# r of eight tiles read in 1536-byte runs and turned by 64x64 products, rstd on ScalarE, a new order

## The chip, the core and the metric

The kernel runs on one core of one Trainium2 chip, in one launch. The metric is the device time of one execution in microseconds, lower is better. The core's engines work side by side, each through its own list of instructions in order: TensorE (PE, with its weight loads PEld), VectorE (DVE), ScalarE (ACT), GpSimd (POOL), and SyncE (SP), whose list here is only the issuing of transfers. ACT also issues a few transfers. All transfers run on the same 16 DMA engines.

## The reference

The first half is a linear attention with a decaying state over 768 time steps, for 4 batches, 8 heads and head size 48. The second half is a normalised two-layer network with a residual.

```python
for t in range(S):
    kt, vt, rt = k[:, :, t], v[:, :, t], r[:, :, t]
    cur = einsum('bhd,bhe->bhde', u[None] * kt, vt)
    y[:, :, t] = einsum('bhd,bhde->bhe', rt, state + cur)
    state = w[None, :, :, None] * state + einsum('bhd,bhe->bhde', kt, vt)
x = y.transpose(0, 2, 1, 3).reshape(B, S, 384)
xn = (x - mean(x)) / sqrt(var(x) + 1e-06) * g_ln
out = x + maximum(xn @ w_ch1, 0) @ w_ch2      # 384 -> 1536 -> 384
```

The inputs r, k, v lie in memory as (batch, head, time, 48), in float32.

## The kernel before

**Tiles.** The 768 steps of each batch are cut into 6 chunks of 128 steps. Tile i is chunk i // 4 of batch i % 4, so there are 24 tiles, and tile i needs the state that tile i - 4 left. Inside a tile the recurrence is written as products over 128 steps, with the powers of w drawn into r and k ahead of them (factor tables Fr and Fk, made once at the start from ln w and exp).

**One tile's way.** The steps are small functions, and each names its tile:

- LR, LK, LV load r, k and v of the tile as (128 tokens, 8 heads, 48), which makes 1024 runs of 192 bytes per load. SR and SK multiply by Fr and Fk into sc in bfloat16 (heads padded to 64). CV copies v to bfloat16.
- TR turns r and k on PE by products with the identity (heads in pairs, 128x128 each, four for r and four for k), and TC, TCr, TCk copy the results from PSUM into trs. For tiles 12 to 23 TKR does both by a DMA transpose instead.
- AT makes the 128x128 scores of each head (16 products of two tiles are one ATP). AM, or its halves AMa and AMb, multiplies them by the causal mask into A on DVE.
- Q multiplies the turned r by the turned k. S makes the bonus (a product with uwI) and the state's gain k^T v, and for tiles 4 to 7 adds the old state by a product with the identity. CC copies the bonus to cc, VB makes Vb = v * cc. ZU and ZD form the new state Z.
- Y makes the output from A and v, and from the turned r and the old Z. X adds Vb into x (fp32) on DVE, with the row sum. SQ squares on ACT, XN makes the centred bfloat16 xn. LT turns xn on PE and XT copies it to xT (LT2 and LTD do it by a DMA transpose). RS makes rstd.
- UP is one piece of the first layer (12 or 6 products into one PSUM bank), RL the relu into hT, DN a third of the second layer (4 products), OT the output with rstd and the residual, STO the store. DA, DB, OA, OB, SA and SB are the halves for the last tile.

Tiles 0 to 5 and 20 to 23 go through the network alone, tiles 6 to 19 in pairs (GROUPS). UP's number is 16 * group + piece.

**Weights.** LW1 loads a third of w_ch1 (768 KB, 2048-byte runs), SW scales a quarter of the columns' rows by the norm's gain and rounds it (three SW per third). LW2 and CW do the same for w_ch2 in the same buffers. LC and WF load w, u and g for the tables; WB, LN, FK, FR, CT, CP, WL build the tables. DU issues PE products on a tile of zeros.

**Order.** The scheduler is off. PLAN is one long list of steps (name, number, engine letter), and walking it fixes each engine's order: `v` is DVE, `s` ACT, `g` POOL, and h, p, o, a choose a PSUM bank. An engine that reaches an instruction whose input isn't there waits, and all that stands behind it on that engine waits too. [...]

```python
for step in PLAN.split():
    name, i, e = step.split(",")
    steps[name](int(i), e)
```

Of the kernel before, what the change touches and what calls it, by code (L numbers as in the profile page):

```python
# [19 lines left out]
DU,7,h SR,0,v TR,0,h TCk,0,s SR,1,v TR,1,h TCk,1,v TCr,0,s Q,0,v AT,0,- CP,0,s WL,0,s LR,2,- SR,2,g TCr,1,v LK,2,- SK,2,g TR,2,h AMb,0,v AMa,0,v  # L20
AT,1,- LV,1,- LK,3,- AMb,1,v AMa,1,v UW,0,g TCk,2,s TCr,2,s AT,2,- AMb,2,v UGC,0,s LV,0,- CV,0,s S,0,h CC,0,v VB,0,v ZU,0,v Y,0,h X,0,v XN,0,v LR,3,-
CV,1,s Q,1,g SK,3,g SR,3,g TR,3,- Q,2,g S,1,o CC,1,v VB,1,g ZU,1,v AMa,2,v Y,1,- X,1,v LK,5,- LR,4,- SR,4,g TCr,3,s TCk,3,s AT,3,- Q,3,v AM,3,v LV,2,-
CV,2,s S,2,h CC,2,s ZU,2,v LT,0,o XN,1,s XT,0,s LK,4,- LR,5,- SR,5,v VB,2,v SK,4,g DU,3,p TR,4,- TC,4,v Q,4,v LV,3,- CV,3,s S,3,o CC,3,s SQ,1,s ZU,3,v
LV,4,- SK,5,g TR,5,- TC,5,s VB,3,g Y,2,- X,2,v LT,1,- XT,1,s XN,2,s CV,4,g S,4,h ZU,4,v CC,4,s LV,5,- CV,5,g ATP,4,- AM,4,v LW1,0,- SW,1,s Y,3,h
SQ,0,s X,3,v XN,3,s SQ,2,s LT,2,h XT,2,v Q,5,g S,5,- AM,5,v ZU,5,v Y,4,o SW,2,g SW,0,g UP,16,- RL,16,s LW1,2,- SW,6,s CC,5,s LT,3,- XT,3,s UP,32,-
RL,32,s UP,0,- RL,0,s LW1,1,- SW,5,s VB,4,g X,4,v XN,4,v SW,7,g SW,8,g UP,2,o RL,2,v VB,5,g UP,48,p RL,48,v Y,5,h SW,3,g LK,6,- SK,6,v X,5,v UP,18,-
RL,18,s XN,5,s SW,4,g UP,49,p RL,49,s UP,33,o LR,7,- SR,7,v UP,34,- RL,34,s LK,7,- SK,7,g RS,2,g RL,33,v UP,17,- RL,17,s TR,7,p TC,7,s RS,0,g LT,5,h
XT,5,v LT,4,- UP,1,o LR,6,- Q,7,v LW2,2,- UP,82,- SR,6,g TR,6,- UP,81,- XT,4,s RL,1,v LV,7,- CV,7,v CW,5,v S,7,- CC,7,v ZU,7,v CW,4,g DN,6,- RL,82,v
# [36 lines left out]
def kernel(  # L65
# [142 lines left out]
    def LC(i, e):  # L208
        if i == 2:
            issuer(e).dma_start(out=rows[2 * HP : NR, :], in_=moe_g_ln.rearrange("(kc p) -> kc p", p=P))  # L210
# [129 lines left out]
    def CV(i, e):  # L340
        copy(e, vv(i)[:], vf(i)[:])
# [321 lines left out]
```

## Time and profile before

| what | value |
|---|---|
| times of three runs | 148.16, 148.97, 151.61 us (median 148.97) |
| profiled execution | 148.24 us, of which the profile's span is 146.5 us |
| PE busy | 135.8 us, 93% of the span |
| DVE busy | 110.5 us, 75% |
| ACT busy | 80.1 us, 55% |
| POOL busy | 94.0 us, 64% |
| DMA | 99267 packets, 94508 of them under 512 bytes; SP's queue 86.3% of 16 engines' span |
| instructions | 4250 |

An engine's busy time is the time in which at least one of its instructions was running. Matmuls overlap, so a mean duration (219 ns for a product with 128 columns) is longer than the distance from one to the next. The span starts with the first recorded instruction and ends with the last store.

### The profile page before, as it was taken

To read this page: it belongs to the slowest core of one execution; us is meant where nothing else is said; L and a number is where in the kernel's file an instruction comes from. 1 tells how busy PE (TensorE), PEld (TensorE's weight loads), DVE (VectorE), ACT (ScalarE), POOL (GpSimd) and SP (SyncE) were. 2 spreads that over 40 slices of the span, in tenths; PEclk is the share of its full clock that TensorE was granted. 3 is DMA by queue.
4 is the path that set the end of the run, shared out by engine and by line. 5 is a ranking of instruction groups with operands and counts; after the bars stand their busy time and mean duration, and the time that the engine had idled before them with its cause. 6 is when DMAs were issued, how large, how long until landed. Compare 5 with 4: busy or idle time off the path is not lost.

```text
span 146.5 us, 4250 instructions
## 1 busy us (share of the span) xinstructions
PE 135.8 (93%) x1693; PEld 108.2 (74%) x1693; DVE 110.5 (75%) x220; ACT 80.1 (55%) x175; POOL 94.0 (64%) x132
## 2 busy tenths in 40 slices
PE   3966699999999999999999999999999999999991
PEld 1455477998687897787688887966877777888871
DVE  4569999767969899985959948897946796875232
ACT  2575577977676467466386560663654752244600
POOL 4089878967888999989957493428553076644030
PEclk9999556999999999999999999999999999999999
DMA  5999899999889999899999999988999997830114
GB/s 97 209 211 221 175 277 401 194 258 380 231 170 188 206 197 232 156 215 242 96 229 206 260 233 186 217 166 185 245 157 199 229 184 156 206 123 0 54 37 182
DMA packets 99267, 28.59 MB, mean 195 GB/s; under 512 B 94508, under 2 KB 97712, under 8 KB 99248
## 3 DMA queue, kind: packets, MB, share of 16 engines
q1 hardware_dynamic: 98352, 27.24, 86.3%
q10 hardware_dynamic: 896, 1.09, 2.0%
q8 instruction: 13, 0.21, 0.6%
q14 instruction: 6, 0.05, 0.1%
HBM read 18.88 MB, written 4.72 MB: 161 GB/s over the span
## 4 chain that ended last, share of the span: by engine, by line
PE 60%; SPq 11%; DMA 11%; DVE 7%; POOL 6%; issue 4%; DVEq 0%; POOLq 0%
PE hp L527 17%; PE o L557 16%; PE s L557 7%; PE s L527 5%; SPq L332 4%; DMA w_f<-in_moe_w_ch_dram 4%; SPq L329 4%; SPq L326 3%; DMA trs<-sc 3%; DMA rf<-in_r_dram 3%; PE o L527 3%; PE at L371 2%; PE hp L452 2%; POOL sc L194 2%; PE at L348 2%
## 5 line engine op out<-in xcount | busy, mean ns | idle before, releaser
L527 PEld LDWEIGHTS <-w_sb 128*128 128x128 bf16 x612 | 47.9, 114 | 2.4 <-POOL w_sb L312 0.4
L527 PE MATMUL hp<-xT,w_sb 128*128 128x128 bf16 (+1 forms) x408 | 39.9, 244 | 0.3 <-POOL w_sb L312 0.3
L557 PEld LDWEIGHTS <-hT 128*128 128x128 bf16 x276 | 25.2, 97 | 13.7 <-issue 0.4
L557 PE MATMUL o<-w_sb,hT 128*128 128x384 bf16 x180 | 34.5, 326 | 0.0
L543 ACT ACTIVATE hT<-hp 128x512 bf16<-128x512 f32 x41 | 24.3, 597 | 18.2 <-PE hp L527 17.7
L381 DVE TENSOR_TENSOR A<-at,mask 128x1024 bf16<-128x1024 f32 (+1 forms) x27 | 28.9, 1096 | 1.2 <-PE at L371 1.2
L194 POOL TENSOR_TENSOR sc<-kf,Fk 128x384 bf16<-128x384 f32 x14 | 14.5, 1044 | 10.5 <-DMA kf<-in_k_dram 10.4
L434 POOL TENSOR_TENSOR Vb<-vf,cc 128x384 f32<-128x384 f32 x17 | 14.7, 868 | 8.7 <-ACT cc L189 3.6
L557 PE MATMUL s<-w_sb,hT 128*128 128x384 bf16 x96 | 18.9, 326 | 0.2 <-DVE x L459 0.2
L194 POOL TENSOR_TENSOR q<-trs 128x512 bf16<-128x512 bf16 x11 | 13.4, 1220 | 5.5 <-PE hp L527 2.6
L194 POOL TENSOR_TENSOR sc<-rf,Fr 128x384 bf16<-128x384 f32 x12 | 13.0, 1082 | 5.3 <-DMA rf<-in_r_dram 5.3
L466 ACT ACTIVATE sqj<-x,sm 128x384 bf16<-128x384 f32 x24 | 14.7, 611 | 1.4 <-DVE x L459 1.3
L615 DVE SCALAR_TENSOR_TENSOR ot<-o,rs,x 128x384 f32<-128x384 f32 x15 | 9.2, 613 | 4.5 <-POOL rs L483 2.8
L459 DVE SCALAR_TENSOR_TENSOR x<-hp,Vb 128x384 f32<-128x384 f32 x19 | 10.5, 554 | 2.3 <-PE hp L452 1.6
L483 POOL TENSOR_TENSOR rs<-rs,expo 128x1 f32<-128x1 f32 (+1 forms) x17 | 10.6, 625 | 1.4
L472 ACT ACTIVATE xn<-x,sm 128x384 bf16<-128x384 f32 x13 | 8.0, 613 | 5.7 <-DVE x L459 5.6
L371 PE MATMUL at<-trs 48*128 48x128 bf16 x192 | 8.6, 229 | 2.4 <-ACT trs L189 1.2
L527 PE MATMUL s<-xT,w_sb 128*128 128x128 bf16 (+1 forms) x120 | 10.8, 235 | 0.0
L194 POOL TENSOR_TENSOR Z<-ZS,WLZ 128x384 bf16<-128x384 f32 x10 | 10.3, 1030 | 0.6 <-DVE ZS L428 0.6
L545 DVE TENSOR_SCALAR hT<-hp 128x512 bf16<-128x512 f32 x9 | 6.2, 689 | 4.6 <-PE hp L527 4.6
L371 PEld LDWEIGHTS <-trs 48*128 48x128 bf16 x192 | 6.0, 99 | 4.9 <-ACT trs L189 2.1
L194 DVE TENSOR_TENSOR sc<-rf,Fr 128x384 bf16<-128x384 f32 x12 | 7.5, 633 | 2.3 <-DMA rf<-in_r_dram 2.2
(116 smaller groups left out, 214.3 us busy)
## 6 DMA issues: line engine op xcount, KB each, us to landing
rf<-in_r_dram SPq DMA_DIRECT2D x24, 192.0 KB, 3.8
kf<-in_k_dram SPq DMA_DIRECT2D x24, 192.0 KB, 3.9
vf<-in_v_dram SPq DMA_DIRECT2D x24, 192.0 KB, 3.9
w_f<-in_moe_w_ch_dram SPq DMA_DIRECT2D x6, 768.0 KB, 7.2
out_dram<-ot SPq DMA_DIRECT2D x18, 192.0 KB, 3.4
out_dram<-ot ACTq DMA_DIRECT2D x5, 192.0 KB, 2.0
trs<-sc SPq DMA_TRANSPOSE x12, 3.9
xT<-xn SPq DMA_TRANSPOSE x9, 2.8
```

The lines of the kernel that those rows point to most:

```text
L194: engines[e].tensor_tensor(out=out, in0=in0, in1=in1, op=ALU.mult)
L371: nc.tensor.matmul(out=t[:, par, q, :], lhsT=trs(i)[p0 : p0 + D, 1, q, :], rhs=trs(i)[p0 : p0 + D, 0, q, :], start=True, stop=True,)
L381: nc.vector.tensor_tensor(out=AA(i)[:, a:b].rearrange("p e q t -> p (e q) t"), in0=psum["at", i][:, a:b].rearrange("p e q t -> p (e q) t") ...
L434: engines[e].tensor_tensor(out=Vb(i)[:].rearrange("p (h d) -> p h d", h=H), in0=vf(i)[:], in1=cc(i)[:].unsqueeze(2).to_broadcast([P, H, D] ...
L459: nc.vector.scalar_tensor_tensor(out=xx(i)[:], in0=psum["y", i][:, :C], scalar=1.0, in1=Vb(i)[:], op0=ALU.mult, op1=ALU.add, accum_out=sm[ ...
L466: nc.scalar.activation(out=sqj[:], in_=xx(i)[:], func=ACT.Square, bias=sm[i][:], scale=-float(C), accum_out=sq[g][:, j : j + 1])
L472: nc.scalar.activation(out=xn(i), in_=xx(i)[:], func=ACT.Identity, bias=sm[i][:], scale=-float(C))
L483: nc.gpsimd.tensor_tensor(out=rs[g][:], in0=rs[g][:], in1=expo[:, :n], op=ALU.pow)
L527: nc.tensor.matmul(out=t[:, a * gw : (a + 1) * gw].rearrange("p (j t) -> p j t", j=size), lhsT=w1_sb[n][kc][:, fb::FB], rhs=xT(g)[:, :size ...
L543: nc.scalar.activation(out=o, in_=s, func=ACT.Relu)
L557: nc.tensor.matmul(out=psum["o", i][:, :C], lhsT=hT(g)[:, fk, j * P : (j + 1) * P], rhs=w2_sb[d][:, a, :], start=(seen == 0 and a == 0), s ...
L615: nc.vector.scalar_tensor_tensor(out=ot(i), in0=psum["o", i][:, :C], scalar=rs[g][:, j : j + 1], in1=xx(i)[:], op0=ALU.mult, op1=ALU.add,)
```

## The change

**Loads of r for tiles 0 to 7.** LR of these tiles reads 1536-byte runs: one run is eight consecutive tokens of one head. The partition is then (group of eight tokens, head), and the free dimension is (token in the group, 48). A load has 128 runs instead of 1024. The tiles 8 to 23, and all of k and v, are loaded as before.

**Turning them.** Because a partition now holds a head, r's factor table has another layout, Fq, made once by the new steps MR, MU, MS, WS, LNQ, FA and FQ (small integer tables, a product with a selection matrix for ln w per partition, Ln, a DVE product, Exp). TR of these tiles is 32 products of 64 rows, 64 weights and 32 columns, instead of r's four 128x128 ones, into a two-bank float32 tile; TCr copies it with a permuted access pattern. k of these tiles is turned by TK (four 128x128 products) and copied by KC. The heads are paired as (q, q + 4) instead of (2q, 2q + 1) throughout, which changes access patterns in SK, SR, CV, CC and Y.

**rstd.** RS moves from POOL (a scale, then a power) to ACT (Ln with scale and bias, then Exp).

**Vb.** VB may run on ACT, as eight products of one head each; five tiles use it.

**Order.** PLAN is a new list. The products on zeros at the start (DU,21, DU,7 and DU,3) are gone, one DU,6 stands ahead of the first UP, and the first table loads come in another order.

```diff
+PACK = 8
+R_PACKED = 8
 PLAN = """
-LR,1,- LK,0,- MI,0,g MW,0,v WF,0,s WB,0,- LC,0,s LC,1,s MM,0,g MP,0,v TL,0,s LC,2,s DU,21,h LN,0,s FK,0,s FR,0,s SK,0,v LK,1,- LR,0,- SK,1,v CT,0,o
+LR,1,- MI,0,g MW,0,v LC,0,s MS,0,v WS,0,- WF,0,s WB,0,h LC,1,s LC,2,s CT,0,o MM,0,g MR,0,g MU,0,v TL,0,s LNQ,0,s FA,0,v LR,0,- MP,0,v FQ,0,s SR,1,v
...
+    def WS(i, e):
+        t = psum["wq"] = bank(e, "p", [P, 512], FP32)
+        for a in range(2):
+            nc.tensor.matmul(
+                out=t[:, :D], lhsT=sel[:, a].rearrange("k p h -> k (p h)"),
+                rhs=rows[:HP, a * DP : a * DP + D], start=(a == 0), stop=(a == 1),
+            )
+    def LNQ(i, e):
+        nc.scalar.activation(out=lnq[:], in_=psum["wq"][:, :D], func=ACT.Ln)
+    def FA(i, e):
+        times(
+            e, Fq[:], lnq[:].unsqueeze(1).to_broadcast([P, PACK, D]),
+            pow_r[:].unsqueeze(2).to_broadcast([P, PACK, D]),
+        )
+    def FQ(i, e):
+        nc.scalar.activation(out=Fq[:], in_=Fq[:], func=ACT.Exp)
...
     def LR(i, e):
+        if i >= R_PACKED:
+            issuer(e).dma_start(out=rf(i)[:], in_=chunk_src(r, i))
+            return
+        c, b = divmod(i, B)
+        issuer(e).dma_start(
+            out=rf(i)[:].rearrange("p j d -> p (j d)"),
+            in_=r[b, :, c * L : (c + 1) * L, :].rearrange("h (p j) d -> p h (j d)", j=PACK),
+        )
     def SR(i, e):
-        times(e, scr(i)[:, :, :D], rf(i)[:], Fr[:])
+        if i < R_PACKED:
+            times(e, scr(i)[:, :, :D], rf(i)[:], Fq[:])
+        else:
+            times(e, paired(scr(i))[:, :, :, :D], plain(rf(i)[:]), plain(Fr[:]))
     def TR(i, e):
...
+        t = psum["tr", i] = ps_a.tile([P, 2, 512], FP32, name="at")
+        n = PACK * HP * LP // 2
+        to = t[:, :, :n].rearrange("p g (j q t) -> p g j q t", j=PACK, q=HP)
+        for j in range(PACK):
+            for a in range(2):
+                for g in range(2):
+                    par = (g + a) % 2
+                    half = slice(g * DP, (g + 1) * DP)
+                    nc.tensor.matmul(
+                        out=to[par * DP : (par + 1) * DP, g, j],
+                        lhsT=scr(i)[half, j, :], rhs=pick[half, par],
+                        start=True, stop=True,
+                    )
+    def TK(i, e):
+        t = psum["tk", i] = bank(e, "a", [P, 2 * HP, P], BF16)
+        flat = sck(i).rearrange("p (q e) d -> p q (e d)", e=2)
+        for q in range(HP):
+            nc.tensor.transpose(out=t[:, q, :], in_=flat[:, q, :], identity=ident[:])
+    def KC(i, e):
+        copy(e, trs(i)[:, 1], psum["tk", i][:, :HP])
     def TCr(i, e):
+        if i < R_PACKED:
+            n = PACK * HP * LP // 2
+            copy(
+                e, trs(i)[:, 0].rearrange("p q (g t j) -> p g q t j", g=2, j=PACK),
+                psum["tr", i][:, :, :n].rearrange("p g (j q t) -> p g q t j", j=PACK, q=HP),
+            )
     def VB(i, e):
+        if e == "s":
+            for h in range(H):
+                nc.scalar.activation(out=o[:, h], in_=vf(i)[:, h], func=ACT.Copy, scale=cc(i)[:, h : h + 1])
     def RS(g, e):
-        nc.gpsimd.tensor_scalar(
-            out=rs[g][:], in0=sq[g][:], scalar1=1.0 / C, scalar2=1e-6 * C * C, op0=ALU.mult, op1=ALU.add
-        )
-        nc.gpsimd.tensor_tensor(out=rs[g][:], in0=rs[g][:], in1=expo[:, :n], op=ALU.pow)
+        nc.scalar.activation(out=rs[g][:], in_=sq[g][:], func=ACT.Ln, bias=eps[:], scale=1.0 / C)
+        nc.scalar.activation(out=rs[g][:], in_=rs[g][:], func=ACT.Exp, scale=-0.5)
```

Three places show how the lists move. The first is SP's list from its tenth load to the third part of w_ch1 (rf, kf, vf are the tiles of r, k, v, the number behind them is the tile; w1_f is a third of w_ch1). Before:

```order
L329 DMA rf3_83<-in_r_dram 128x8x48
L326 DMA kf5_74<-in_k_dram 128x8x48
L329 DMA rf4_84<-in_r_dram 128x8x48
L332 DMA vf2_93<-in_v_dram 128x8x48
L326 DMA kf4_73<-in_k_dram 128x8x48
L329 DMA rf5_85<-in_r_dram 128x8x48
L332 DMA vf3_94<-in_v_dram 128x8x48
L332 DMA vf4_95<-in_v_dram 128x8x48
L332 DMA vf5_96<-in_v_dram 128x8x48
L301 DMA w1_f0_243<-in_moe_w_ch1_dram 128x3x512
L301 DMA w1_f2_245<-in_moe_w_ch1_dram 128x3x512
L301 DMA w1_f1_244<-in_moe_w_ch1_dram 128x3x512
```

And of the change:

```order
L385 DMA rf3_83<-in_r_dram 128x1x384
L378 DMA kf4_73<-in_k_dram 128x8x48
L391 DMA vf1_92<-in_v_dram 128x8x48
L391 DMA vf2_93<-in_v_dram 128x8x48
L391 DMA vf3_94<-in_v_dram 128x8x48
L378 DMA kf5_74<-in_k_dram 128x8x48
L385 DMA rf5_85<-in_r_dram 128x1x384
L391 DMA vf5_96<-in_v_dram 128x8x48
L353 DMA w1_f2_251<-in_moe_w_ch1_dram 128x3x512
L353 DMA w1_f1_250<-in_moe_w_ch1_dram 128x3x512
L385 DMA rf6_86<-in_r_dram 128x1x384
L353 DMA w1_f0_249<-in_moe_w_ch1_dram 128x3x512
```

Ahead of the first third of w_ch1 stand 18 loads of 1024 runs before, and 11 of them with 6 of 128 runs in the change; v of tile 4 moved behind the weights.

The second place is DVE's first work behind the memsets, up to the first masked scores (A0 is the masked score tile of tile 0; trs0 is r and k of tile 0 turned). Before:

```order
L194 TENSOR_TENSOR sc0_102<-kf0_69,Fk_232 128x8x48
L194 TENSOR_TENSOR sc1_103<-kf1_70,Fk_232 128x8x48
L194 TENSOR_TENSOR sc0_102<-rf0_80,Fr_231 128x8x48
L194 TENSOR_TENSOR sc1_103<-rf1_81,Fr_231 128x8x48
L191 COPY trs1_113<-hp_325 128x512
L194 TENSOR_TENSOR q0_117<-trs0_112 128x512
L191 COPY trs1_113<-hp_325 128x512
L381 TENSOR_TENSOR A0_120<-at_337,mask_228 128x512 x2
```

And of the change:

```order
L206 TENSOR_TENSOR sc1_103<-rf1_81,Fq_235 128x8x48
L206 TENSOR_TENSOR sc0_102<-kf0_69,Fk_239 128x2x4x48
L203 CAST trs0_112<-at_322 128x2x4x64
L206 TENSOR_TENSOR sc2_104<-rf2_82,Fq_235 128x8x48
L203 COPY trs0_112<-s_391 128x512
L206 TENSOR_TENSOR q0_117<-trs0_112 128x512
L203 COPY trs1_113<-hp_470 128x512
L480 TENSOR_TENSOR A0_120<-at_476,mask_228 128x512 x2
```

The copies of the two turned halves of tile 0 and of k of tile 1 (L203) now stand between the products, and the first masked scores stand behind k of tile 1. On PE the turns of tiles 0, 1, 4 and 2 and k of tiles 0 and 1 stand ahead of tile 0's scores.

The third place is DVE just ahead of the first relu of the network (hT is the relu's output, x the attention's output). Before:

```order
L459 SCALAR_TENSOR_TENSOR x3_143,sm3_170<-hp_591,Vb3_139 128x384
L191 COPY xT2_159<-hp_604 128x384
L381 TENSOR_TENSOR A2_122<-at_579,mask_228 128x1024
L194 TENSOR_TENSOR Z5_133<-s_610,WLZ_241 128x384
L459 SCALAR_TENSOR_TENSOR x4_144,sm4_171<-o_622,Vb0_136 128x384
L474 TENSOR_SCALAR xn2_156<-x4_144,sm4_171 128x384
L545 TENSOR_SCALAR hT0_161<-o_694 128x4x128
```

And of the change:

```order
L480 TENSOR_TENSOR A0_120<-at_667,mask_228 128x1024
L203 CAST trs0_112<-at_679 128x2x4x64
L564 SCALAR_TENSOR_TENSOR x2_142,sm2_169<-s_716,Vb2_138 128x384
L564 SCALAR_TENSOR_TENSOR x3_143,sm3_170<-o_730,Vb3_139 128x384
L480 TENSOR_TENSOR A1_121<-at_741,mask_228 128x1024
L206 TENSOR_TENSOR Z3_131<-hp_657,WLZ_247 128x384
L480 TENSOR_TENSOR A2_122<-at_750,mask_228 128x1024
L647 TENSOR_SCALAR hT0_161<-hp_811 128x4x128
```

Before, PE's first UP (UP,16, bank hp) stands behind Y of tiles 0 to 4 and S of tiles 0 to 5. In the change the first UP (UP,2) stands behind Y of tiles 0 to 3 and S of tiles 0 to 3, and it writes bank o, which X of tile 3 (x3 above) reads.

More of the change, by code (lines that the diff above doesn't have):

```diff
@@ L21 @@
[L21 to L28, printed above, removed]
@@ L93 @@
     FB = FW // P
+    LP = L // PACK
+    assert H == PACK and H * LP == P
     assert D <= DP and H % 2 == 0 and S % L == 0 and C % P == 0 and F % (P * NW) == 0
@@ L161 @@
     one = const.tile([1, P], FP32, name="one")
-    ln_all = const.tile([P, H, D], FP32, name="ln_all")
+    ln_all = Fr
     NR = 2 * HP + CK
@@ L254, in MP @@
         nc.vector.memset(uwI[:], 0.0)
-        nc.vector.memset(expo[:], -0.5)
+        nc.vector.memset(eps[:], 1e-6 * C * C)
     def DU(i, e):
```

155 lines of the change are left out of this document (98 added, 57 removed).

## The prediction

> **What bounds the kernel now.** I read the slices of the span first, then the busy time in windows, then the chain that ended last.
>
> ```profile
> span 146.5 us, 4250 instructions
> PE   3966699999999999999999999999999999999991
> PEclk9999556999999999999999999999999999999999
> ```
>
> From the seventh slice on (22 us) PE is busy almost without a break up to the last slice. Before that it is half idle, and in slices 5 and 6 it runs at half clock. So the time is made of the moment at which the dense stretch begins, PE's own work behind it, the gaps in it, and a tail. The windows have, behind the stretch and its length, the busy time of PE, PEld, DVE, ACT and POOL (with instructions), the granted clock, the DMA share and GB/s:
>
> ```profile
> 10.00:15.00 5.00, 2.75 (x57) 2.28 (x56) 4.93 (x12) 3.22 (x9) 4.58 (x5) 0.90 1.07 210
> 15.00:20.00 5.00, 3.96 (x42) 2.97 (x43) 5.00 (x12) 2.47 (x8) 3.97 (x5) 0.50 0.89 179
> 20.00:25.00 5.00, 4.83 (x75) 3.92 (x72) 4.88 (x12) 3.94 (x10) 4.34 (x6) 0.58 1.02 381
> 25.00:30.00 5.00, 4.90 (x93) 4.91 (x94) 4.18 (x9) 4.34 (x11) 4.36 (x7) 1.00 0.96 220
> 70.00:80.00 10.00, 9.46 (x125) 7.83 (x124) 7.99 (x14) 5.72 (x16) 7.92 (x11) 1.00 1.21 177
> ```
>
> Two resources are full from 10 to 25 us: DVE (4.93, 5.00 and 4.88 of 5) and the DMA engines (1.07, 0.89 and 1.02). The window from 70 us has PE's longest idle time in the dense stretch, 0.54 us.
>
> ```profile
> 16.70 0.98 SPq L332
> 17.72 5.84 DMA w_f<-in_moe_w_ch_dram
> 25.10 0.86 PE hp L527 x12
> 142.48 1.00 PE o L574 x12
> ```
>
> The first UP (L527) starts at 25.10 us. By the chain it was released by w_ch1, whose load SP issued at 17.72 behind 18 loads. PE ends at 143.48, and the last 3.0 us of the span are one DVE product and the last store. Nothing in the change shortens that tail, since OA,23 and SA,23 still end the lists.
>
> DVE would have allowed UP only a little earlier, though. Its rows in the stretch:
>
> ```profile
> 9.64 0.41 DVE L191 COPY trs<-hp 128x512 bf16<-128x512 bf16 x1
> 9.98 3.07 DVE L381 TENSOR_TENSOR A<-at,mask 128x512 bf16<-128x512 f32 x5
> 12.97 0.15 DVE L191 COPY cc<-hp 128x8 f32<-128x8 f32 x1
> 13.15 0.56 DVE L434 TENSOR_TENSOR Vb<-vf,cc 128x384 f32<-128x384 f32 x1
> 13.63 0.55 DVE L194 TENSOR_TENSOR Z<-hp,WLZ 128x384 bf16<-128x384 f32 x1
> 14.10 0.55 DVE L459 SCALAR_TENSOR_TENSOR x<-hp,Vb 128x384 f32<-128x384 f32 x1
> 14.69 0.42 DVE L474 TENSOR_SCALAR xn<-x,sm 128x384 bf16<-128x384 f32 x1
> 16.63 0.70 DVE L194 TENSOR_TENSOR q<-trs 128x512 bf16<-128x512 bf16 x1
> 17.25 1.21 DVE L381 TENSOR_TENSOR A<-at,mask 128x1024 bf16<-128x1024 f32 x1
> 18.39 0.54 DVE L194 TENSOR_TENSOR Z<-hp,WLZ 128x384 bf16<-128x384 f32 x1
> L545 DVE TENSOR_SCALAR hT<-hp 128x512 bf16<-128x512 f32 x9 | 6.2, 689 | 4.6 <-PE hp L527 4.6
> ```
>
> From one start to the next I take the real price of a DVE step in this stretch: a half mask (12.97 - 9.98) / 5 = 0.60, Vb 0.48, Z 0.47, X 0.59, Q 0.62, a whole mask 1.14, a copy of turned k 0.41, cc 0.15.
>
> **The change part by part.**
>
> *Loads.* A load of 192 KB at the 210 GB/s of the window from 10 us takes 0.94 us. The w_ch1 loads, with 2048-byte runs, move at 381 GB/s, which would make 0.52 us for the same 192 KB; for 1536-byte runs there is no row, and the ends are 0.52 and 0.94. I take the lower, as its runs are the nearer in size. Ahead of w_ch1 six loads of r save 6 x 0.42 = 2.5 us, and v of tile 4 moves behind it (0.94), so w_ch1 is issued and lands some 3.4 us earlier. That is hidden: what is late next is DVE, worked out here.
>
> *The start of the attention.* Fq has a longer chain than Fk had:
>
> ```profile
> 0.71 0.55 ACTq L204 DMA_DIRECT2D w_row<-in_w_dram  x1
> 0.80 0.17 DVE L225 MEMSET rows<- 11x128 f32 x1 [0.80 <-PEq L647]
> 1.16 0.73 DVE L252 MEMSET sc<- 128x128 uint32 x5
> 1.91 0.38 DVE L253 MEMSET WLZ<- 128x384 f32 x1
> 2.78 1.28 ACT L230 ACT_TABLE_LOAD   x1 [2.78 <-DVE expo L255]
> 2.82 0.42 ACTq L210 DMA_DIRECT2D rows<-in_moe_g_ln_dram  x1
> 4.67 0.61 ACT L277 ACTIVATE Fk<-ln_all,pow_i 128x384 f32<-128x384 f32 x1
> 7.32 1.06 PE L348 MATMUL hp<-ident,sc 128*128 128x128 bf16 x16
> L194 POOL TENSOR_TENSOR sc<-rf,Fr 128x384 bf16<-128x384 f32 x12 | 13.0, 1082 | 5.3 <-DMA rf<-in_r_dram 5.3
> ```
>
> ACT's first issue now waits for the memset of rows (ends at 0.97 instead of a start at 0.71, +0.3), and the fourth issue (0.42) comes ahead of the table load, which therefore ends at 2.78 + 1.28 + 0.7 = 4.8. Then come Ln of 48 columns (below the 0.61 of Fk; say 0.3), FA on DVE (0.56, as Vb), FQ (0.61) and SR,0 on POOL (1.08): the first turn can start at about 7.4. The first transposes of before started at 7.32. So this part costs nothing, but the masked scores and all that follows wait for more PE work than before.
>
> *The turns.* No row shows a 64x64 product with 32 columns. The nearest:
>
> ```profile
> 22.97 0.50 PE L452 MATMUL hp<-vv,A 128*128 128x48 bf16 x8
> 32.54 0.45 PE s L348 x8
> 37.08 0.55 PE at L371 x16
> 37.63 0.76 PE s L557 x4
> 39.06 0.65 PE o L557 x4
> 40.36 0.17 PE hp L444 x4
> 40.53 0.20 PE hp L452 x8
> 42.18 0.08 PE hp L402 x4
> ```
>
> Products with 48 columns take 0.20 / 8 = 25 ns each at full clock. At half clock eight of them lasted 0.50 us, of which about 0.19 is the run-out of the last, so (0.50 - 0.19) / 7 = 44 ns. Transposes take 0.45 / 8 = 56 ns, and 16 at the start 1.06 / 16 = 66 ns. The 48-row score products (34 ns each) also show that a change of the array's shape costs something: four DN behind them took 0.76 instead of 0.65 us, 0.11 more. I take 27 ns at full clock and 44 at half, with 0.11 per turn: these turns are nearest to the 48-column products. A turn is then 32 x 0.027 + 0.11 = 0.97 us, or 32 x 0.044 + 0.11 = 1.52 us at half clock. The bounds are 25 ns below and 56 (66 at half clock) above.
>
> Ahead of the first masked score PE must do the turns of tiles 0, 1, 4 and 2 and k of tiles 0 and 1. The products on zeros that warmed the clock are gone (they ran from 3.84 us, and by 7.32 the transposes were at full rate), so I put the first two turns and the first k at half clock: 2 x 1.52 + 0.62 + 2 x 0.97 + 0.45 = 6.05. With 0.25 for the last result and 0.41 for KC,1 the first mask starts at 7.4 + 6.05 + 0.25 + 0.41 = **14.1 us, against 9.98 before**. DVE stands idle for part of that.
>
> *DVE from there to the first UP.* UP,2 writes the bank that X,3 reads, and stands on PE behind Y,3. DVE's list up to X,3: six half masks 3.60, two Vb 0.96, four X 2.36, three Z 1.41, two Q 1.24, two KC 0.82, one cc 0.15, one whole mask 1.14, one TCr from float32 PSUM (as a relu, 0.69): 12.4 us. So X,3 ends at 26.5 and UP,2 starts at about **26.7, 1.6 us later than 25.10**. ACT and POOL were less full in this stretch (2.47 and 3.97 of 5 us from 15 us), and the weights are there.
>
> *PE work behind the first UP.* Less of the attention is done by then. Added are S of tiles 4 and 5 with the old state (16 small products 4 x 0.08 / 2 = 0.16, k^T v 2 x 0.17 as the 96-column products of L444, two products of 384 columns 2 x 0.16), Y of one more tile (0.17 + 0.20), one LT (3 x 0.056 = 0.17), less 8 transposes (0.45): +0.9. The turns of tiles 6 and 7 come on top: 2 x 0.97 = 1.9. Sum **+2.8 us**, all on the engine that sets the end.
>
> *The rest.* RS on ACT, Vb on ACT and the other engine letters move work between engines that have room in the dense stretch (in the window from 70 us DVE 80%, ACT 57%, POOL 79%). I price them at nothing. Where an Ln and Exp, or eight small products, delay a relu that PE waits for, it costs up to a microsecond; where POOL's relief feeds PE sooner, up to 0.5 is won. The earlier loads end 8 x 0.42 = 3.4 us of transfer time; PE's gaps of that kind are 0.54 us at most in that window, and I leave them in.
>
> Sum, against the profiled execution's 148.24 us: 148.24 + 1.6 + 2.8 = **152.6 us**. That run lies 0.7 us below the median of the three runs shown (148.97).
>
> A rule of the Trainium skill speaks against the change. Its page "TensorEngine Tiling" (Restrictions, Key Properties) says that column tiling switches off the fast weight load and that changing the tiling mode drains the engine; "TensorE: Matmul & The Clock Gate" (LDWEIGHTS) gives columns / 1.2 ns for a plain load, by which I estimate 64 / 1.2 = 53 ns per product and 1.7 us per turn. By that the sum would be close to the first rival's. The drain agrees with the trace (0.76 against 0.65 us). The load no row here shows; the first page also says that separate tiles load and multiply in parallel, which would leave my sum as it is.
>
> **Rivals.**
>
> *Each product pays for its own load.* At the transposes' 66 and 56 ns a turn is 2.22 or 1.90 us. The first mask starts at 14.1 + 2 x 0.70 + 2 x 0.93 = 17.4, and the two later turns cost 1.9 more: 152.6 + 3.3 + 1.9 = 157.8 us. For it speaks that every product loads new weights, against it that neighbours here use different quarters of the array, as the score products use different halves (34 ns).
>
> *DVE is never starved, and the kernel isn't slower.* If the turns overlap well enough, DVE runs its list without a break from the end of its memsets (about 6.9 us: FA ends at 5.7, then the memsets of sc and WLZ, 0.73 + 0.38). Ahead of the first mask it has three products, a TCr, two KC and a Q, 3 x 0.5 + 0.69 + 0.82 + 0.62 = 3.6. So the first mask is at 10.5, UP,2 at 23.1, 2.0 earlier; with 2.7 more work for PE and the 0.5 us of waiting for transfers won the time is 148.24 - 2.0 + 2.7 - 0.5 = 148.4. For it: DVE did run unbroken from 9 to 25 us before. The point from which it decides is a first mask at 13.4 us: later than that the time is over 2% above the median. I have 14.1, so it is close.
>
> *The weights were the bound.* If UP followed w_ch1, it would start 3.4 us earlier: 148.24 - 3.4 + 2.8 = 147.6. Against it stands DVE's list, which ends no sooner than 23.1. This would be the change doing what its loads suggest.
>
> **How the numbers follow.** My forecast has 0.50, from 150.5 to 155 us with 152.6 the likeliest; the full load price 0.17, the unstarved DVE 0.25, the weights 0.03. To be faster by over 2%, which is about what a measurement of this kernel can tell from no change, UP would have to start before 20 us, below DVE's unbroken list: 0.05. A fourth of the forecast's chance (0.12) lies under 151.95, so within 2% is 0.25 + 0.03 + 0.12 = 0.40 and slower 0.55. The range goes from 148.0 to 157.6; outside it lie the weights, the faster case and the upper part of the load case, together under 0.2.
>
> **What would show it.** Right: the first mask row on DVE at about 14 us, DVE full from there to 26, the first UP at 26 to 27 and w_ch1 waiting unused from about 20; eight groups of 32 products of about 1 us. Wrong: UP before 24 us or starting just behind w_ch1's scaling, turns of 2 us and more, or a dense stretch of PE with new gaps, where relus or outputs wait for ACT.

## The result, and the profile after

| | median | lowest to highest | runs |
|---|---|---|---|
| before | 148.82 us | 148.16 to 151.61 | 4 |
| with the change | 152.27 us | 151.81 to 152.73 | 4 |

The ratio is 1.027, with a 95% interval from 1.022 to 1.032: slower. The profiled execution took 152.19 us. Ratios here and below are against the kernel before on the same chip and leave out slow executions (over 1.5% above the fastest of their kernel); the profiles of two experiments (turns issued twice, products on zeros) are of slow executions, so only rows of single groups are used from them.

The slices of the span, as for before:

```profile
span 150.4 us, 4736 instructions
PE   2777799998979999999999998999999998999992
PEclk9999999999999999999999999999999999999999
```

PE is busy from the sixth slice on, as before (whose sixth slice has a 9, too), but there are more slices below 9 behind it. Next the start, on PE (start, duration, line, shapes, count, and the idle time ahead with what ended it) and on DVE:

```profile
6.46 1.04 PE L427 MATMUL at<-pick,sc 64*64 64x32 bf16 x64 [0.82 <-POOL sc L206]
7.44 0.61 PE L437 MATMUL s<-ident,sc 128*128 128x128 bf16 x4
11.05 2.48 DVE L480 TENSOR_TENSOR A<-at,mask 128x512 bf16<-128x512 f32 x4
23.55 0.56 DVE L564 SCALAR_TENSOR_TENSOR x<-o,Vb 128x384 f32<-128x384 f32 x1
24.23 1.11 PE L629 MATMUL o<-xT,w_sb 128*128 128x128 bf16 x12
28.23 0.43 PE L427 MATMUL at<-pick,sc 64*64 64x32 bf16 x32
28.59 0.86 PE L629 MATMUL hp<-xT,w_sb 128*128 128x128 bf16 x12
```

The first two turns begin at 6.46, the first mask at 11.05, and the first UP (L629) at 24.23, behind X of tile 3 (23.55). So the dense stretch begins 0.87 us **earlier** than before (25.10). It ends at 147.45. The same stretch of before and of after, with the busy time of PE, PEld, DVE, ACT and POOL:

```profile
25.10:143.48 118.38, 117.31 (x1477) 95.34 (x1477) 90.25 (x170) 65.52 (x143) 77.11 (x102) 1.00 0.89 191
```

```profile
24.23:147.45 123.22, 119.65 (x1568) 97.12 (x1566) 97.86 (x183) 72.64 (x202) 68.90 (x76) 1.00 0.88 187
```

It is 4.84 us longer: PE is busy 2.34 us more (119.65 - 117.31) and idle 2.50 us more (3.57 instead of 1.07). With the start, 148.24 - 0.87 + 4.84 = 152.2, which is the profiled time. What PE waited for (in total, times, longest):

```profile
PE o L659 <- ACT w_sb L201: 1.0, 1, 1.0
PE hp L629 <- DVE ot L717: 0.7, 1, 0.7
PE hp L614 <- DVE xn L579: 0.6, 1, 0.6
PE o L629 <- DMA xT<-xn: 0.6, 1, 0.6
PE hp L629 <- POOL w_sb L364: 0.4, 1, 0.4
```

No single wait is large, and each is for another step: the scaled w_ch2, an output, an xn, a DMA transpose, the second third of w_ch1. In the dense stretch of before, none of PE's waits was over 0.3 us. The chain that ended last passes through the first of them, and shows how it came about:

```profile
23.27 7.31 DMA rf<-in_r_dram
34.10 0.59 SPq L370
34.74 7.57 DMA w_f<-in_moe_w_ch_dram
42.33 0.84 ACT w_sb L201
43.21 0.81 PE o L659 x4
```

A third of w_ch2 (L370) was issued from 34.10 on, its transfer ended at 42.31 (34.74 + 7.57), its cast on ACT at 43.17, and the first DN that needs it started at 43.21.

### The profile page after: what moved, and what is told of

It reads as the page before. It is cut to its first block, busy times and chain, and to the rows that moved or that the text cites. A ratio compares the mean times of both kernels' runs of the same rounds, so it can differ in the third digit from the quotient of the medians.

```text
span 150.4 us, 4736 instructions
## 1 busy us (share of the span) xinstructions
PE 137.4 (91%) x1911; PEld 110.1 (73%) x1911; DVE 118.8 (79%) x236; ACT 86.6 (58%) x233; POOL 86.7 (58%) x109
## 3 DMA queue, kind: packets, MB, share of 16 engines
q1 hardware_dynamic: 91184, 27.24, 84.4%
## 4 chain that ended last, share of the span: by engine, by line
PE 55%; DMA 20%; SPq 13%; DVE 5%; POOL 2%; issue 2%; ACT 1%; DVEq 0%; POOLq 0%
PE hp L629 16%; PE o L659 13%; DMA rf<-in_r_dram 9%; PE s L659 8%; DMA w_f<-in_moe_w_ch_dram 5%; SPq L378 5%; PE s L629 4%; SPq L391 4%; DMA trs<-sc 3%; PE o L629 3%; DMA xT<-xn 3%; PE at L470 3%; POOL sc L206 2%; SPq L385 2%; DVE A L480 2%
## 5 line engine op out<-in xcount | busy, mean ns | idle before, releaser
L629 PEld LDWEIGHTS <-w_sb 128*128 128x128 bf16 x612 | 48.8, 114 | 4.6 <-DMA xT<-xn 2.0
L629 PE MATMUL hp<-xT,w_sb 128*128 128x128 bf16 (+1 forms) x384 | 37.1, 245 | 1.1 <-DVE ot L717 0.7
L645 ACT ACTIVATE hT<-hp 128x512 bf16<-128x512 f32 x29 | 16.9, 593 | 22.4 <-PE hp L629 21.7
L659 PE MATMUL s<-w_sb,hT 128*128 128x384 bf16 x108 | 21.3, 326 | 0.0
L206 POOL TENSOR_TENSOR sc<-kf,Fk 128x384 bf16<-128x384 f32 x17 | 18.7, 1102 | 3.2 <-DMA kf<-in_k_dram 3.2
L579 POOL TENSOR_SCALAR xn<-x,sm 128x384 bf16<-128x384 f32 x10 | 6.4, 645 | 14.4 <-DVE x L564 14.4
L647 DVE TENSOR_SCALAR hT<-hp 128x512 bf16<-128x512 f32 x18 | 12.1, 687 | 3.0 <-PE hp L629 2.9
L629 PE MATMUL s<-xT,w_sb 128*128 128x128 bf16 (+1 forms) x132 | 11.6, 234 | 0.0
L206 POOL TENSOR_TENSOR Vb<-vf,cc 128x384 f32<-128x384 f32 x12 | 9.9, 832 | 0.9 <-ACT xT L201 0.8
L629 PE MATMUL o<-xT,w_sb 128*128 128x128 bf16 (+1 forms) x96 | 9.4, 245 | 0.6 <-DMA xT<-xn 0.6
L539 ACT ACTIVATE Vb<-vf,cc 128x48 f32<-128x48 f32 x40 | 9.5, 320 | 0.7 <-DVE cc L203 0.6
L717 DVE SCALAR_TENSOR_TENSOR ot<-s,rs,x 128x384 f32<-128x384 f32 x9 | 5.5, 610 | 4.3 <-DMA out_dram<-ot 2.4
```

The costliest lines, as they stand in the source:

```text
L206: engines[e].tensor_tensor(out=out, in0=in0, in1=in1, op=ALU.mult)
L539: nc.scalar.activation(out=o[:, h], in_=vf(i)[:, h], func=ACT.Copy, scale=cc(i)[:, h : h + 1])
L629: nc.tensor.matmul(out=t[:, a * gw : (a + 1) * gw].rearrange("p (j t) -> p j t", j=size), lhsT=w1_sb[n][kc][:, fb::FB], rhs=xT(g)[:, :size ...
L645: nc.scalar.activation(out=o, in_=s, func=ACT.Relu)
L647: nc.vector.tensor_relu(out=o, in_=s)
L659: nc.tensor.matmul(out=psum["o", i][:, :C], lhsT=hT(g)[:, fk, j * P : (j + 1) * P], rhs=w2_sb[d][:, a, :], start=(seen == 0 and a == 0), s ...
```

## The experiments

Three theories stood at the beginning: that the new **order** costs (O), that the **packing and its turns** cost (T), or that **RS on ScalarE** does (R).

**w_ch2 earlier.** The thirds of w_ch2 are loaded in the order of before, and two of them go past a load on SP's list each.

```diff
-LR,7,- ... LK,8,- ... LW2,0,- CW,1,g CW,0,s DN,0,- DN,4,p LW2,2,- CW,4,s CW,5,g ... LW2,1,-
+LW2,2,- LR,7,- ... LW2,1,- LK,8,- ... CW,5,g CW,4,s DN,2,- DN,6,p CW,2,s CW,3,g ... LW2,0,-
```

> The changed kernel with one thing moved: the loads of w_ch2 are issued two steps earlier on SP's list each (the thirds in the order 2, 1, 0, as before the change, and the first products of tiles 0 and 1 renumbered to match). Theory O (the new order opens gaps in the dense stretch, the largest being PE's wait of 1.0 us at 43.2 us for the scaled w_ch2): that wait goes and the time falls by 1 to 1.5 us from 152.3, to 151. Theory T (the price is PE's work and the start of the attention, the turns above all): 152.3 within 0.4, the wait turns up elsewhere.

Measured: 153.76 us, ratio 1.037 (1.029 to 1.045). Neither theory had this. The issue rows of w_ch2, of after and of this run, and this run's new waits:

```profile
L370 SPq DMA_DIRECT2D w_f<-in_moe_w_ch_dram x3: 430/432/1792, 32.9 to 35.2; - x3
```

```profile
L373 SPq DMA_DIRECT2D w_f<-in_moe_w_ch_dram x3: 632/2924/3852, 24.1 to 37.4; - x3
34.13 0.43 PE L430 MATMUL at<-pick,sc 64*64 64x32 bf16 x32 [1.16 <-POOL sc L209]
40.99 0.33 PE L517 MATMUL o<-vv,sc 128*128 128x96 bf16 x4 [1.53 <-POOL vv L206]
```

The wait for the scaled w_ch2 is gone, but issuing an early third now holds SP for 2.9 and 3.9 us (median and longest, 0.4 and 1.8 in after), and behind it a load of r and one of v come late: PE waits 1.16 us for the product of that r, ahead of a turn, and 1.53 us for the cast of that v. The hold itself is not new, since in the change the load of that r held SP for 4.25 us in the same place (from 23.27); new is that 768 KB stand ahead of it, and its product starts at 33.09 instead of 30.65. The gap was only moved, and it grew.

**Plain loads in the new order.** r of tiles 0 to 7 by 192-byte runs and 128x128 transposes; the steps MR, MU, MS, WS, LNQ, FA and FQ are left out.

```diff
-R_PACKED = 8
+R_PACKED = 0
-... TL,0,s LNQ,0,s FA,0,v LR,0,- MP,0,v FQ,0,s SR,1,v
+... TL,0,s LN,0,s FK,0,s FR,0,s LR,0,- MP,0,v SR,1,v
```

> The changed kernel's order with r of tiles 0 to 7 loaded plainly (192-byte runs) and turned by 128x128 transposes; the steps that only the packed form needs (the power table by token, the picking matrices) are left out. RS and VB stay on ScalarE. Theory O (the order costs): 151.5 to 152.5, no faster than the changed kernel. Theory T (the packing and its turns cost): about 149, as before the change. If the 1536-byte runs do save transfer time, the first UP starts over 2 us later here than at 24.2 and the time is above 153.

Measured: 151.49 us, ratio 1.022 (1.014 to 1.030). The lower end of theory O. Its dense stretch, and the issue of w_ch1 here and in after:

```profile
25.08:146.67 121.59, 119.35 (x1512) 96.87 (x1509) 98.61 (x183) 72.97 (x202) 69.99 (x77) 1.00 0.91 184
15.79 1.53 SPq L356 DMA_DIRECT2D w_f<-in_moe_w_ch_dram  x2
```

```profile
15.81 1.20 SPq L353 DMA_DIRECT2D w_f<-in_moe_w_ch_dram  x2
```

The first UP starts as in before (25.08), and the dense stretch is 3.2 us longer without any turn in it. So most of the loss goes with the order and the engines that it uses, not with the packing. And w_ch1 is issued at 15.8 us with either kind of load: what brought it forward from 17.72 is the order, not the 1536-byte runs. (This start is not that of before: the factor table waits for a row that is fetched later here, and the transposes begin at 8.90.) What they cost at the start, four per tile for two tiles and then the next group:

```profile
8.90 1.03 PE L420 MATMUL at<-ident,sc 128*128 128x128 bf16 x8 [3.15 <-POOL sc L209]
9.73 0.63 PE L440 MATMUL s<-ident,sc 128*128 128x128 bf16 x4
```

That is (9.73 - 8.90) / 2 = 0.42 us a tile, where a turn in the change took (7.44 - 6.46) / 2 = 0.49.

**The old order with packed loads.** TR and TK in banks of their own, RS on GpSimd as in before.

```diff
-... DU,7,h SR,0,v TR,0,h TCk,0,s SR,1,v TR,1,h TCk,1,v ...
+... DU,7,h SR,0,v TR,0,- TK,0,h KC,0,s SR,1,v TR,1,- TK,1,h KC,1,v ...
```

> The order of before, with packed loads of r and the turns of tiles 0 to 7 in it (turns of r and transposes of k in banks of their own, RS on GpSimd as before). Theory O: as fast as before or faster, 147.5 to 149.2, since packing alone costs only eight turns of 0.45 us against eight groups of four transposes. Theory T: 150 to 152.5.

Measured: 152.96 us, ratio 1.032 (1.024 to 1.040). Theory T's number, but only in a part of T's place, the start of the attention:

```profile
14.69 1.90 DVE L483 TENSOR_TENSOR A<-at,mask 128x512 bf16<-128x512 f32 x3 [0.71 <-PE at L473]
29.45 1.09 PE L635 MATMUL hp<-xT,w_sb 128*128 128x128 bf16 x12
29.45:147.55 118.10, 117.07 (x1538) 95.76 (x1534) 89.62 (x170) 65.24 (x144) 75.15 (x101) 1.00 0.88 182
```

The dense stretch is as short as in before (118.1). The whole loss lies ahead of it: the first UP comes at 29.45, 4.4 us late. About 2 us of that is there before any turn: the product for the old tables stands on PE behind the one for the new table (WS) and starts at 4.07 instead of 2.30, and the first turn starts at 9.38 where the first transposes of before started at 7.32. Then DVE stands idle behind PE, 0.86 us ahead of its first copy (11.40) and 0.71 among its first masks, and the first mask comes at 12.71 instead of 9.98. So the starved DVE of the prediction is real here, in the order that was not made for the turns, with 1.6 us of the 4.4.

**RS on ScalarE in the old order.**

```diff
-        nc.gpsimd.tensor_scalar(out=rs[g][:], in0=sq[g][:], ...)
-        nc.gpsimd.tensor_tensor(out=rs[g][:], in0=rs[g][:], in1=expo[:, :n], op=ALU.pow)
+        nc.scalar.activation(out=rs[g][:], in_=sq[g][:], func=ACT.Ln, bias=eps[:], scale=1.0 / C)
+        nc.scalar.activation(out=rs[g][:], in_=rs[g][:], func=ACT.Exp, scale=-0.5)
```

> The kernel before with one change: RS as Ln and Exp on ScalarE in place of the two GpSimd operations. My price of nothing: 148.8 within 0.5. Theory R (the seventeen pairs of 0.5 us hold up relus that PE waits for): 149.8 or more.

Measured: 151.32 us, ratio 1.020 (1.012 to 1.027). Theory R. RS itself is short (two instructions of 0.29 and 0.20 us); the reading is in who waits for it. For the instructions that use rs, the idle time ahead of them, and then PE's waits for the output step:

```profile
  ACT rs L480: 4.4, 5
PE o L554 <- DVE ot L612: 0.8, 2, 0.5
PE o L524 <- DVE ot L612: 0.7, 1, 0.7
```

OT on DVE waited five times, 4.4 us in all, for an rs that was still behind other work in ACT's list, and PE waited 1.5 us for OT, because the next DN needs its bank. In before the same rows have 2.8 us in four for POOL's rs, and 0.3 us of PE:

```profile
  POOL rs L483: 2.8, 4
PE o L402 <- DVE ot L615: 0.3, 1, 0.3
```

That is 1.2 of the 2.9 us. The first UP is 0.55 us later (25.65), 0.5 lies behind PE's last product, and the rest in smaller waits.

The next question was whether these prices belong to the parts or to the pairing of part and order.

**RS back on GpSimd in the new order.**

```diff
-        nc.scalar.activation(out=rs[g][:], in_=sq[g][:], func=ACT.Ln, bias=eps[:], scale=1.0 / C)
-        nc.scalar.activation(out=rs[g][:], in_=rs[g][:], func=ACT.Exp, scale=-0.5)
+        nc.gpsimd.tensor_scalar(out=rs[g][:], in0=sq[g][:], ...)
+        nc.gpsimd.tensor_tensor(out=rs[g][:], in0=rs[g][:], in1=expo[:, :n], op=ALU.pow)
```

> The changed kernel with one thing undone: RS by the two GpSimd operations, at the same places of the lists. In the old order RS on ScalarE alone cost 3.2 us, by OT on VectorE standing behind it. Theory R (the same holds in the new order): 149 to 150.5. Theory N (the new order was made for RS on ScalarE, so undoing it only trades one wait for another): 152.3 within 1.

Measured: 162.71 us, ratio 1.095 (1.083 to 1.106). Theory R falls here: in this order the same step costs 10 us when it is taken **off** ScalarE. POOL's row shows why, and PE's largest wait what it did:

```profile
110.41 1.01 POOL L206 TENSOR_TENSOR sc<-rf,Fr 128x384 bf16<-128x384 f32 x1
116.19 0.19 POOL L585 TENSOR_SCALAR rs<-sq 128x2 f32<-128x2 f32 x1 [4.76 <-ACT sqj L571]
118.16 0.99 POOL L206 TENSOR_TENSOR sc<-kf,Fk 128x384 bf16<-128x384 f32 x1
PE at L470 <- DMA trs<-sc: 4.8, 1, 4.8
```

RS stands in the list right behind SQ. On ACT it follows SQ in the same queue and waits for nothing. On POOL it waits 4.76 us for that SQ, and the product of k with Fk behind it, which feeds a DMA transpose, is late; PE then waits 4.8 us. That wait is about half of the price. From the first UP to the end of PE's work, PE is idle 5.3 us more than in the change and busy 3.4 us more, in part because behind the wait its products go at half pace (16 score products take 1.04 us at 122.42, and 0.55 in the dense stretch of before; the granted clock is 0.66 from 121 to 126 us).

**The new start and the old rest.** Packed; the new order up to the first load of w_ch1, then the remaining steps as in before, RS on GpSimd.

```diff
-... VB,3,g X,3,v ATP,4,- AM,4,v XN,1,s LT,1,p LW1,2,- SQ,1,s RS,1,s SW,8,s ...
+... VB,3,g X,3,v ATP,4,- AM,4,v XN,1,s LT,1,p Q,4,v SQ,1,s ZU,3,v LV,4,- XT,1,s XN,2,s ...
```

> Packed loads and turns, the new order up to the first load of w_ch1, and from there the remaining steps in the order of before, RS on GpSimd. The old order's dense stretch took 118.1 us with packing and 118.4 without, the new order's 123.2; the new order with packing starts its first UP at 24.2. Theory D (the new order's loss lies behind the first UP, in the order of the dense stretch): 148 to 150. Theory T (packing costs wherever it stands): 151 or more.

Measured: 153.48 us, ratio 1.033 (1.022 to 1.044). A miss for theory D, and in the range of theory T:

```profile
25.53 0.26 PE L504 MATMUL hp<-uwI,q 128*128 128x2 bf16 x4 [1.52 <-DVE q L209]
27.98 1.45 PE L635 MATMUL hp<-xT,w_sb 128*128 128x128 bf16 x12
```

The old rest has the bonus of tiles 4 and 5 and Y of tile 4 ahead of the first UP, and by the new start DVE comes late to the Q that the first of them needs. PE waits 1.52 us, and UP begins at 27.98.

**The same list with plain loads.**

```diff
-R_PACKED = 8
+R_PACKED = 0
```

> The same list of steps as the run with the new start and the old rest, with plain loads of r and 128x128 transposes. The pair gives the price of packing alone. By the traces so far it is within 1 us: eight turns of 0.36 to 0.55 us against eight groups of four transposes of 0.23 to 0.41, and at the start a first UP 0.9 earlier with packing. Theory T: 2 us or more in favour of plain loads.

Measured: 152.50 us, ratio 1.026 (1.017 to 1.034). Packing costs about 1 us in this pair, within its uncertainty, so theory T does not explain the loss either. The dense stretch of the two runs, packed and plain, says where it lies:

```profile
28.01:148.37 120.36, 118.47 (x1537) 96.66 (x1534) 89.94 (x170) 65.99 (x147) 75.25 (x102) 1.00 0.86 179
```

```profile
28.81:147.55 118.74, 117.61 (x1482) 96.36 (x1479) 89.05 (x170) 66.29 (x148) 75.89 (x102) 0.99 0.87 182
```

With the old rest the stretch takes 120.4 and 118.7 us, near the 118.4 of before, and PE is idle in it for 1.9 and 1.1 us, where the change has 123.2 and 3.6. On this point theory D holds: the gaps of the change belong to the order of its later steps and the engines they use, not to its start, its loads or its pairing of the heads, which this packed run shares with it. The time is no better because the old rest has more to do ahead of the first UP.

**The new order alone,** with both of the edits above: plain loads, RS on GpSimd.

```diff
-R_PACKED = 8
+R_PACKED = 0
-        nc.scalar.activation(out=rs[g][:], ...)
+        nc.gpsimd.tensor_scalar(out=rs[g][:], ...)
```

> The new order with plain loads of r and with RS on GpSimd: the order without the two other parts (VB stays on ScalarE for five tiles). With RS on ScalarE it took 151.5. Theory R: 148.5 to 149.5, the order itself costs next to nothing. Theory D (the order costs): 151 or more.

Measured: 160.98 us, ratio 1.075 (1.057 to 1.092). It has the same wait as the run with RS on GpSimd above: PE waits for a DMA transpose once, for 4.9 us.

The runs side by side:

| order | RS on | r plain | r packed |
|---|---|---|---|
| before's | GpSimd | 1 | 1.032 (1.024 to 1.040) |
| before's | ScalarE | 1.020 (1.012 to 1.027) | not run |
| new | ScalarE | 1.022 (1.014 to 1.030) | 1.027 (1.022 to 1.032), the change |
| new | GpSimd | 1.075 (1.057 to 1.092) | 1.095 (1.083 to 1.106) |
| mixed | GpSimd | 1.026 (1.017 to 1.034) | 1.033 (1.022 to 1.044) |

In no order did packing gain; its price goes from 0.5% to 3.2%. In the new and the mixed order that price is rather too low, because the plain loads start there with a late factor table (PE waits 3.15 us ahead of its first transposes, 0.82 ahead of the first turns). The new order with its own engine for RS costs 2.2% without packing. The parts do not add up: RS on ScalarE costs 2.0% in one order and saves over 5% in the other.

The last runs took single terms.

**Every turn issued twice.**

```diff
-        for j in range(PACK):
+        for j in [j for _ in range(2) for j in range(PACK)]:
```

> The changed kernel with every turn issued twice in a row into the same place (64 products instead of 32; the values are the same). The traces so far show a turn at 0.54 us where PE runs at half clock and 0.36 at full clock, the prediction had 1.52 and 0.97. By the traces: the first mask comes 2 turns later at least (0.5 to 1.1 us), the two turns of tiles 6 and 7 add 0.7 in the dense stretch, so 153 to 154.5, less where PE waits anyway. By the predicted price: 156 or more.

Measured: ratio 1.038 (1.027 to 1.049), some 1.6 us above the change, as the traces had it, though the two intervals overlap. The rows give the price itself:

```profile
6.46 1.90 PE L427 MATMUL at<-pick,sc 64*64 64x32 bf16 x128 [0.90 <-POOL sc L206]
31.20 0.69 PE L427 MATMUL at<-pick,sc 64*64 64x32 bf16 x64
31.82 0.86 PE L629 MATMUL hp<-xT,w_sb 128*128 128x128 bf16 x12
```

At the start 64 more products add 1.90 - 1.04 = 0.86 us, 13 ns each, 0.43 us per turn. In the dense stretch a doubled turn occupies PE for 0.62 us (31.20 to 31.82) where a single one took 0.36 (28.23 to 28.59): 0.26 us for 32 products, 8 ns each, and 0.1 once per turn. Against the transposes of r that it replaces (0.42 us at the start) a turn costs nearly nothing.

**VB on GpSimd** for the five tiles that have it on ScalarE.

```diff
-VB,8,s ... VB,11,s ... VB,16,s ... VB,19,s ... VB,20,s
+VB,8,g ... VB,11,g ... VB,16,g ... VB,19,g ... VB,20,g
```

> The changed kernel with VB of tiles 8, 11, 16, 19 and 20 on GpSimd instead of ScalarE, at the same places of the lists; RS stays on ScalarE. If VB behaves as RS did in this order (10 us for putting it back, since what stands behind it on GpSimd is then late): 155 or more. If only a step that waits on ScalarE's own result does that, and VB waits for cc alone: 152.3 within 1.

Measured: 154.15 us, ratio 1.038 (1.030 to 1.045). Between the two expectations, with a new wait of PE for a Q product that DVE makes late:

```profile
59.94 0.20 PE L504 MATMUL hp<-uwI,q 128*128 128x2 bf16 x2 [1.41 <-DVE q L209]
```

On DVE the X ahead of that Q waits 1.41 us for a Vb that POOL now makes. So eight small products on ACT per tile (320 ns each) are not slower here than one on POOL.

**w_ch1 earlier in the kernel before,** the one try at a faster kernel.

```diff
-CC,0,v ... XN,0,v ... LV,5,- CV,5,g ATP,4,- AM,4,v LW1,0,-
+CC,0,s ... XN,0,s ... ATP,4,- AM,4,v LW1,0,- LV,5,- CV,5,g
```

> The kernel before with two small moves: the load of v of tile 5 (with its cast) behind the first load of w_ch1, and XN,0 and CC,0 from VectorE to ScalarE. The first UP of before follows w_ch1 (23.6 us) and VectorE's list (X,3 at 24.3). If these two set the start: w_ch1 lands 0.9 earlier, first UP at 24.3 to 24.7, and 147.6 to 148.3 where before has 148.8. If the lists are so tightly fitted that any move opens a wait, as in the runs so far: 149.5 to 152.

Measured: 149.17 us, ratio 1.005 (1.001 to 1.010). No gain. What it opened:

```profile
14.92 0.61 ACT L475 ACTIVATE xn<-x,sm 128x384 bf16<-128x384 f32 x1 [2.08 <-DVE x L462]
15.98 0.48 PE L418 MATMUL o<-vv,sc 128*128 128x96 bf16 x4 [1.28 <-ACT vv L192]
26.43 0.84 PE L530 MATMUL hp<-xT,w_sb 128*128 128x128 bf16 x12
```

ACT waits 2.08 us at the moved XN, the cast of v behind it is late, PE waits 1.28 us for it, and the first UP comes at 26.43 instead of 25.10. Of all kernels run, the one before stays the fastest.

**Products on zeros ahead of WS,** in the change.

```diff
-MS,0,v WS,0,-
+MS,0,v DU,16,o WS,0,-
```

> The changed kernel with four products on zeros (512 columns each) ahead of WS on TensorE, so that it is busy from 1 us on. If they bring the first turns and transposes to full clock, as in the old order (a turn 0.36 us, four transposes 0.40 instead of 0.61), the first mask comes about 1 us earlier than 11.05, and the time falls by up to 1 us, to 151.3. If TensorE is throttled later for it, or VectorE's list sets the first UP anyway: 152.3 within 0.5.

Measured: ratio 1.018 (1.009 to 1.027); its interval overlaps that of the change, so this is inconclusive. The mechanism did not act, since the first two turns took 1.04 us as in the change:

```profile
6.54 1.04 PE L430 MATMUL at<-pick,sc 64*64 64x32 bf16 x64 [0.81 <-POOL sc L209]
```

## Why the prediction was right, and where not

The total, 152.6, came out at 152.27, but two of its terms were wrong by over 2 us, with opposite signs. That the total was met is luck.

- **The start of the attention, 7.4 us.** The first turn began at 6.46. Right in its main point: the longer chain of Fq costs nothing in this order (in the old one the first turn came 2 us later than the first transposes of before).
- **The turns, 0.97 us (1.52 at half clock).** This step failed. They took 0.36 and about 0.5 us. I took the distance of products that use the whole array (25 and 44 ns), and measured were 8 and 13 ns for products that each use a quarter. The bounds (25 to 66 ns) did not hold the value either: the lower one, too, was a price of the whole array, and the 66 is no price of half clock (the 16 transposes at 7.32 went at the full rate; at half pace one takes 0.83 / 8 = 104 ns, by the run with plain loads). The Trainium skill's page "TensorEngine Tiling" (Key Properties) says that tiles load and multiply independently; here the trace agrees (a weight load lasts 139 ns in the mean, and one product follows another after 8 to 13). The 53 ns per load that I estimated from the Trainium skill's page "TensorE: Matmul & The Clock Gate" (LDWEIGHTS) is not what a row shows for these tiles.
- **The first mask at 14.1.** Measured 11.05, by that term and the earlier start. This lies ahead of the 13.4 from which I let the rival of the unstarved DVE decide, and the start went its way: first mask 11.05 for its 10.5, first UP 24.23 for its 23.1.
- **DVE's list, 12.4 us to the end of X,3, and UP behind it.** Right: 11.05 to 24.11 is 13.1 us, of which DVE is busy 12.47, and the first UP followed at 24.23. Q was longer than the 0.62 I took when a POOL instruction was running as it began (the first row; POOL's product ran from 15.86 to 17.18, and Q ended at 17.47), and shorter when none was:

```profile
16.25 1.22 DVE L206 TENSOR_TENSOR q<-trs 128x512 bf16<-128x512 bf16 x1
18.67 0.45 DVE L206 TENSOR_TENSOR q<-trs 128x512 bf16<-128x512 bf16 x1
```

- **First UP +1.6.** Measured -0.87, from the two points above.
- **PE work behind it +2.8.** PE's busy time grew by 2.34. The two turns in it are 0.7 instead of 1.9, the rest 1.6 instead of 0.9. The products that I counted for that rest are the right ones, by the counts of the two stretches; 0.28 us more is the first UP, which went slower (0.95 instead of 0.67).
- **"I price them at nothing", and gaps left in.** The second step that failed. PE's idle time in the stretch grew by 2.50 us. The waits are those of the new order: w_ch2, outputs, xn, a DMA transpose. New gaps in the dense stretch were one of my signs of being wrong, and this one came. That a change of engine is free where the engine has room is refuted twice: RS on ScalarE alone cost 2.0% with ACT 55% busy, and taking it off ScalarE in the new order cost 6.6%. What I looked at was the room of the engine; what counted was the place in its queue.
- **Loads.** w_ch1 was issued 1.9 us earlier, not 3.4, and the pair with plain loads shows that none of it came from the longer runs. Hidden it was, as I said, in the first piece, but by little: its scaling ended at 23.76, and X,3 at 24.11. The second third of w_ch1 kept PE waiting 0.4 us.

With the turns at their true price and gaps at nothing, my sum would have been 148.24 - 0.9 + 1.6 = 149, inside the range but on the wrong side of 2%. The forecast was right only because a term too large stood for a term left out. The 1.6 here is 0.9 + 2 x 0.36.

Open remains the last 0.4 us of PE's busy time, and which of the many moved steps opens which gap: the one gap that was closed opened others.

## What to carry to other kernels

In a kernel whose engines work down fixed lists, the price of moving a step to another engine is not its duration but what it waits for there and what stands behind it: put a step behind its own producer in the same queue, and look for its consumers before looking at the share of busy time. A new order has to be priced as a whole, by its gaps. Where no row shows a shape, let the lower bound come from the smallest thing that the shape could cost, here a quarter of the array at work, not from its nearest relative.

## What the runs showed of the hardware

- Products of 64 rows, 64 weights and 32 columns in the four quarters of the array follow each other after 13 ns at the start and 8 ns in the dense stretch, although each loads new weights.
- The granted clock of the record did not tell PE's pace at the start. Eight score products (48x128) took 0.40 us at 10.11 in before and 0.61 us at 10.40 after the change, both with a granted clock of 1.00 in their slices:

```profile
10.11 0.40 PE L371 MATMUL at<-trs 48*128 48x128 bf16 x8
15.11 0.61 PE L371 MATMUL at<-trs 48*128 48x128 bf16 x8 [0.50 <-ACT trs L189]
```

```profile
10.40 0.61 PE L470 MATMUL at<-trs 48*128 48x128 bf16 x8
```

- At 15.11 eight of them take 0.61 us in before too, and there its record shows 0.50. What lifts the pace was not settled. In before products on zeros run from 3.84, and from 7.32, 3.5 us later, transposes follow each other at the full rate; in the change UP reaches the full rate some 0.6 us behind its start (12 products in 25.18 - 24.23 = 0.95 us, where 12 at full rate take 0.67; 0.6 us is an estimate from these two). In the run with products on zeros ahead of WS, PE had products under way from 1.11 to 5.73 us almost without a break, and the turns at 6.54 still took 1.04 us. The Trainium skill's page "TensorE: Matmul & The Clock Gate" (Part 1: The HAM clock gate) has half rate as the default and some 3.4 us of activity as what lifts it; the 3.5 us of before agree; the recorded 1.00 does not, nor do the 4.6 us of that run, if its products count as activity.
- A Q on DVE that begins while a POOL instruction runs ends 0.27 to 0.29 us behind that instruction, and its length follows from that: in the change 17.47 behind 17.18, 38.82 behind 38.53, 58.94 behind 58.66. With POOL idle it takes 0.41 (at 95.12).
- The longer runs did not settle how much transfer time they save. SP's queue took 84.4% of 150.4 us with packed loads (126.9) and 88.7% of 149.6 us with plain ones (132.7) in the new order, but in the old order 129.0 us packed (85.7% of 150.5) and 126.4 plain (86.3% of 146.5). With RS on GpSimd it was 124.2 packed and 128.9 plain in the new order, 127.2 and 128.5 in the mixed one.
